# KV times wo for two head groups at once, in 64x64 TensorE tiles, on Trainium2

## The chip, the cores and the metric

The kernel runs on one core of a Trainium2 chip. The metric is device time in microseconds (us), the median of the runs. Five engines work side by side: TensorE (PE; its weight loads are listed as PEld), VectorE (DVE), ScalarE (ACT), GpSimd (POOL) and SyncE (SP), which here only issues DMAs.

## The reference, cut to what matters

One transformer block with adaptive layernorm: a linear attention block and a gated feed-forward block, on 2048 tokens of width 1024, 32 heads of 32, feed-forward width 3584, all bf16.

```python
mod = (_silu(c) @ w_mod).reshape(c.shape[0], 6, 1, -1)
sa, ca, ga, sb, cb, gb = (mod[:, 0], ..., mod[:, 5])
h = _layernorm(x) * (1 + ca) + sa
# A: linear attention
q, k, v = split of h @ wqkv into 32 heads of 32
phi = lambda t: jnp.where(t > 0, t + 1, jnp.exp(t)) + 1e-06
pq, pk = (phi(q), phi(k))
kv = jnp.einsum('bhsd,bhse->bhde', pk, v)
z = jnp.einsum('bhsd->bhd', pk)
num = jnp.einsum('bhqd,bhde->bhqe', pq, kv)
den = jnp.einsum('bhqd,bhd->bhq', pq, z)[..., None] + 1e-06
x = x + ga * ((num / den) @ wo)
# B: feed-forward
h = _layernorm(x) * (1 + cb) + sb
x = x + gb * (_gelu(h @ w_gate) * (h @ w_up) @ w_down)
```

## The kernel before, in words

The 32 heads stand in 8 groups of four, 128 columns each. The kernel never forms `num`. It multiplies each group's masked 128x128 KV matrix by the group's 128 rows of `wo` (already scaled by `ga`) and gets W2, 8 tiles of 128x1024. The attention output of a chunk of 128 tokens is then the scaled `pq` times W2, summed over the 8 groups (`wo_mm`, L1266).

The stages, in the order of TensorE:

1. Up to about 127 us: layernorm, the `k` and `q` products and `phi` of both.
2. The M stage, about 127 to 191 us. M is `pk`-transposed times the normalised input, 24 tiles (`m_tile`, L895) of 341 or 342 columns, accumulated over 16 chunks in PSUM banks 0 to 3 in turn. A DMA transpose (`m_t`, `mT`) turns a group's M, and `kv_prod` (L913) multiplies it by the group's columns of `wv` into bank 4 or 5. VectorE masks the result with the block-diagonal `BMASK` into `KVT` (L917). `w2_pair` (L1196) multiplies `KVT` by `WO` into two banks, two matmuls of 128x512, and ScalarE copies both banks to `W2` (L1198). Beside that `wofold` (L1202) scales `WO` by `GAB`, a broadcast row of modulation values; `den` (L1223, bank 5) gives the denominators, whose reciprocals go through DRAM and come back broadcast as `RB` (`rb_load`, L1243); `pq_scale` (L1256, notes `ps`) multiplies them into `pq`. `mod_rows` (L840) sums modulation rows over the partitions with a 32-column stationary operand, at four column positions, in bank 5 or 6.
3. The tail of the M stage, about 191 to 204 us: the first three token chunks of `wo_mm` (banks 0 and 1, 2 and 3, 4 and 5) are written out by hand between the last `kv_prod` and `w2_pair` calls.
4. The rest of `wo_mm` up to about 255 us, partly between feed-forward products. After a chunk, VectorE adds it to `x` (L1274), ScalarE and GpSimd make the second layernorm, and a DMA transpose brings it to the layout of the feed-forward products.
5. The feed-forward products (L1440) and the down projection (L1654), to the end.

`HOOK` puts named steps behind numbered M tiles: `kv3` is `kv_prod` of group 3, `w3` a `w2_pair`, `modp` the modulation rows of the second block, `gbr` the row of `gb`, `rb0.0` a load of `RB`.

The order on TensorE and on SP is the order in which the program is written. For VectorE, ScalarE and GpSimd, `reorder` is a planner over stages 1 to 3 (from the last `k` products to where the feed-forward code begins). It simulates all engines with `COST` (occupation and latency, looked up by the letters of an operation's note, (0.3, 0.1) where there is none), works out due times from the end back, and orders these three engines by due time among what is ready. A stream runs strictly in its order on the chip. DMAs of SP use 8 semaphores in turn, so each waits for the eighth before it.

`WO` lies where `wq` was, and `W2` where `wv` was. Before, `wo` comes in two loads of four groups each.

Of the kernel before, what the change touches and what calls it, by code (L numbers as in the profile page):

```python
# [18 lines left out]
NG = 8  # L19
# [24 lines left out]
OFF_WK = OFF_YT  # L44
# [126 lines left out]
class Sched:  # L171
# [41 lines left out]
    def dma(self, stream, fn, rd=(), wr=(), deps=(), note="", overwrite_ok=False):  # L213
# [6 lines left out]
        if prev is not None:  # L220
# [110 lines left out]
def bass_adaLN_cond__linear_attn_block__geglu_ffn__prompt_kernel(  # L331
# [18 lines left out]
    with ExitStack() as es:  # L350
# [30 lines left out]
        W2 = at("w2", [P, NG, D], bf16, OFF_WK)  # L381
# [63 lines left out]
        def r_sm(name):  # L445
            return [(SMO[name], SMO[name] + SMSZ[name], name)]
# [33 lines left out]
        def r_wo(g, c0=0, c1=D):  # L480
            return [(OFF_WQ + g * 2048 + c0 * 2, OFF_WQ + g * 2048 + c1 * 2, "wo")]
# [22 lines left out]
        def r_w(off, name, dc, c0=0, c1=D):  # L504
            return [(off + (dc * D + c0) * 2, off + (dc * D + c1) * 2, name)]
# [46 lines left out]
        sch = Sched()  # L552
# [356 lines left out]
        def kv_prod(g, bank):  # L909
            i = g % 2  # L910
            o = None
            for dc in range(NDC):
                o = sch.op(T, lambda e, dc=dc: e.matmul(PS(bank, 0, P), WV[:, g, dc, :], MTB[i][:, dc, :],  # L913
                                                        start=(dc == 0), stop=(dc == NDC - 1)),
                           rd=r_wv(g) + r_mtb(i), pwr=(pr(bank) if dc == 0 else ()), note=f"kv g{g} dc{dc}")
            pset_writer(bank, o)
            sch.op(V, lambda e: e.tensor_tensor(KVT[:, g, :], PS(bank, 0, P), BMASK[:, :], ALU.mult), prd=pr(bank), rd=r_sm("bmask"),  # L917
                   wr=r_kvt(g, g + 1), note=f"kvt{g}")

        bank_i = [0, 4]  # L920

# [268 lines left out]
            sch.op(V, lambda e: e.tensor_tensor(Z32[:], BM32[:], ZCOLS[:, :].unsqueeze(2).to_broadcast([P, NG, NH]), ALU.mult),  # L1190
                   rd=r_sm("bm32") + r_sm("zcols"), wr=r_sm("z32"), note="z32")

        def w2_pair(g, b0=6):
            for half in range(2):
                b = b0 + half
                sch.op(T, lambda e, b=b, half=half: e.matmul(PS(b), KVT[:, g, :], WO[:, g, half * 512:(half + 1) * 512], start=True, stop=True),  # L1196
                       rd=r_kvt(g, g + 1) + r_wo(g, half * 512, (half + 1) * 512), pwr=pr(b), note=f"w2 {g}.{half}")
            sch.op(A, lambda e: e.activation(W2[:, g, :], ps_all[:, b0 * 512:(b0 + 2) * 512], ACTF.Copy),  # L1198
                   prd=pr(b0) + pr(b0 + 1), wr=r_w(OFF_WK, "w2", g), note=f"w2cp{g}")
# [61 lines left out]
        def wo_mm(c_, b0, gs):  # L1261
            sg, ci = divmod(c_, CPG)
            last = [None, None]
            for g in gs:
                for half in range(2):
                    last[half] = sch.op(T, lambda e, g=g, half=half: e.matmul(  # L1266
                        PS(b0 + half), PQ[sg][:, g, ci * P:(ci + 1) * P], W2[:, g, half * 512:(half + 1) * 512],
                        start=(g == 0), stop=(g == NG - 1)),
                        rd=r_pq(sg, g, g + 1, ci * P, (ci + 1) * P) + r_w(OFF_WK, "w2", g, half * 512, (half + 1) * 512),
                        pwr=(pr(b0 + half) if g == 0 else ()), note=f"wo c{c_} g{g} h{half}")  # L1270
# [39 lines left out]
        for n, (g, k) in enumerate(tiles):  # L1310
# [656 lines left out]
```

## Time and profile before

| what | before |
|---|---|
| median of 3 runs | 783.46 us (783.44 to 783.54) |
| the profiled execution: time, span of its records | 783.52 us, 781.7 us |
| granted TensorE clock | 1.00 |
| PE busy | 774.5 us, 99% of the span |
| DVE busy | 641.9 us, 82% |
| ACT busy | 376.3 us, 48% |
| L1196 (KVT times WO) | 16 matmuls of 128x512, first at 149.3 us, last at 200.7 us |
| L917 (mask) | 8 instructions of 128x128, median 286 ns |
| L1202 (fold of `ga` into wo) | 8 instructions of 128x1024, median 1218 ns |
| L1205 (wo loads) | 2 of 1024 KB, 7.8 us to landing |
| VectorE busy between 120 and 205 us | 65.4 us |

Times within the execution count from the start of its span. Matmuls are pipelined: a matmul's listed duration reaches into the next one, so what one costs is read from one start to the next.

### The profile page before, as it was taken

The page shows a single profiled execution, that of the slowest core. Times are in us where ns is not written, and L with a number is a line of the kernel's source. Part 1 is how long each engine was busy: PE and PEld are TensorE (multiplying, and loading weights), DVE is VectorE, ACT ScalarE, POOL GpSimd, SP SyncE. Part 2 cuts the span into 40 slices and gives each one's busy share as a digit, 9 for nine tenths or more (in the row PEclk, how much of TensorE's full clock was granted, in tenths as well). Part 3 has the DMA queues.
Part 4 walks back from the last instruction along what each step waited for, and adds up shares of the span by engine and source line. Part 5 has one row for each costly group of instructions (what it writes and reads, how often), then busy time and mean ns, then how long its engine had stood idle before and what let it go on. Part 6 is the DMA issues. An engine that isn't in the chain of part 4 may idle for free.

```text
span 781.7 us, 10762 instructions
## 1 busy us (share of the span) xinstructions
PE 774.5 (99%) x3867; PEld 497.4 (64%) x3867; DVE 641.9 (82%) x954; ACT 376.3 (48%) x631; POOL 47.0 (6%) x126
## 2 busy tenths in 40 slices
PE   8999999999999999999999999999999999999998
PEld 4444445666445667677676767677676576677766
DVE  6699988896689877787989888888989888676767
ACT  2497743243566487778655565555555211111111
POOL 2031300000331012100000000000000000000000
DMA  9879749939999247867353866435356334444331
GB/s 289 250 166 252 156 84 260 229 70 182 216 270 248 82 128 215 226 184 214 93 152 107 246 207 180 141 102 160 94 150 218 112 115 152 145 141 123 113 128 60
DMA packets 196844, 130.22 MB, mean 167 GB/s; under 512 B 69420, under 2 KB 182324, under 8 KB 195768
## 3 DMA queue, kind: packets, MB, share of 16 engines
q1 hardware_dynamic: 196776, 129.55, 61.0%
q8 instruction: 30, 0.49, 0.3%
q14 instruction: 22, 0.18, 0.1%
q10 hardware_dynamic: 16, 0.00, 0.0%
HBM read 92.55 MB, written 23.35 MB: 148 GB/s over the span
## 4 chain that ended last, share of the span: by engine, by line
PE 97%; SPq 1%; DMA 1%; DVE 0%; issue 0%; DVEq 0%
PE ps_all L1440 45%; PE ps_all L1654 21%; PE ps_all L895 7%; PE ps_all L1266 7%; PE ps_all L931 7%; PE ps_all L880 6%; PE ps_all L1575 1%; DMA wmq<-in_w_mod_dram 1%; SPq L598 1%; SPq L603 1%; PE ps_all L913 0%; PE ps_all L1196 0%; SPq L592 0%; PE ps_all L1223 0%; PE ps_all L766 0%; PE ps_all L840 0%
## 5 line engine op out<-in xcount | busy, mean ns | idle before, releaser
L1440 PE MATMUL ps_all<-ss,tp 128*128 128x512 f32 x896 | 214.3, 396 | 0.0
L1440 PEld LDWEIGHTS ps_all<-ss,tp 128*128 128x128 f32 x896 | 168.3, 188 | 37.7 <-DVE ss L1395 0.3
L1654 PE MATMUL ps_all<-dt,sb 128*128 128x512 f32 x424 | 102.5, 398 | 0.0
L1440 PE MATMUL ps_all<-h2a,wt 128*128 128x512 bf16 x448 | 101.6, 380 | 0.0
L1463 ACT ACTIVATE ge<-ps_all 128x512 f32<-128x512 f32 x112 | 64.1, 597 | 73.8 <-DVE ps_all L1451 62.0
L1654 PEld LDWEIGHTS ps_all<-dt,sb 128*128 128x128 f32 x424 | 79.6, 188 | 18.4 <-DVE sb L1630 0.3
L1458 DVE TENSOR_TENSOR ps_all<-ps_all,es 128x512 f32<-128x512 f32 x54 | 37.5, 699 | 49.7 <-ACT es L1448 49.3
L1470 DVE TENSOR_TENSOR ys<-ge,ps_all 128x512 bf16<-128x512 f32 x112 | 74.4, 684 | 3.4 <-PE ps_all L1654 0.5
L1440 PEld LDWEIGHTS ps_all<-h2a,wt 128*128 128x128 bf16 x448 | 37.9, 97 | 57.2 <-ACT ps_all L1445 16.9
L1415 DVE TENSOR_TENSOR tp<-wt 128x1024 fp32r<-128x1024 bf16 x56 | 68.1, 1216 | 2.1 <-DMA wt<-in_B_w_up_dram 2.1
L1415 DVE TENSOR_TENSOR tp<-wt,tp 128x1024 fp32r<-128x1024 bf16 x56 | 68.2, 1219 | 0.0
L880 PE MATMUL ps_all<-wk,h1T 128*128 128x512 bf16 x248 | 56.7, 379 | 0.3 <-DVE h1T L724 0.2
L931 PE MATMUL ps_all<-h1T,wq 128*128 128x512 bf16 x256 | 56.7, 379 | 0.0
L1266 PE MATMUL ps_all<-w,pq 128*128 128x512 bf16 x256 | 56.3, 379 | 0.0
L1440 PE MATMUL ps_all<-ar,tp 128*128 128x512 f32 x224 | 55.5, 390 | 0.0
L869 ACT ACTIVATE eb<-ps_all 128x512 f32<-128x512 f32 x64 | 36.3, 593 | 37.7 <-PE ps_all L880 15.3
L1654 PE MATMUL ps_all<-wd,ya 128*128 128x512 bf16 x212 | 48.5, 380 | 0.0
L1440 PEld LDWEIGHTS ps_all<-ar,tp 128*128 128x128 f32 x224 | 42.1, 188 | 8.8
L1445 ACT ACTIVATE ps_all<-ps_all 128x512 f32<-128x512 f32 x56 | 32.6, 582 | 27.1 <-PE ps_all L1440 27.1
L931 PEld LDWEIGHTS ps_all<-h1T,wq 128*128 128x128 bf16 x256 | 24.9, 98 | 30.0
L1266 PEld LDWEIGHTS ps_all<-w,pq 128*128 128x128 bf16 x256 | 24.7, 98 | 29.9 <-ACT w L1198 0.3
L1625 ACT ACTIVATE sb<-ya 128x896 fp32r<-128x896 bf16 (+1 forms) x16 | 14.5, 913 | 58.8 <-PE ps_all L1654 58.8
(140 smaller groups left out, 977.5 us busy)
## 6 DMA issues: line engine op xcount, KB each, us to landing
wt<-in_B_w_gate_dram SPq DMA_DIRECT2D x28, 512.0 KB, 4.1
wt<-in_B_w_up_dram SPq DMA_DIRECT2D x28, 512.0 KB, 5.3
scr_y<-ys SPq DMA_DIRECT2D x28, 512.0 KB, 3.2
ya<-scr_y SPq DMA_DIRECT2D x14, 896.0 KB, 5.9
rb<-scr_rd SPq DMA_DIRECT2D x32, 256.0 KB, 6.9
wd<-in_B_w_down_dram SPq DMA_DIRECT2D x7, 1024.0 KB, 7.9
wmst<-in_w_mod_dram SPq DMA_DIRECT2D x6, 1024.0 KB, 5.7
wmq<-in_w_mod_dram SPq DMA_DIRECT2D x8, 512.0 KB, 6.8
```

Of the source, the lines that this page charges most:

```text
L869: sch.op(A, lambda e: e.activation(EB[i][:, :], PS(bank), ACTF.Exp), prd=pr(bank), wr=rng, note=f"{note}.exp")
L880: o = sch.op(T, lambda e, dc=dc: e.matmul(PS(bank), H1[sg][:, ci, dc, :], W_[:, dc, jg * 512:(jg + 1) * 512], start=(dc == 0), stop=(dc == ...
L895: o = sch.op(T, lambda e, c_=c_: e.matmul(PS(bank, 0, n), PK[c_][:, g * P:(g + 1) * P], xrow(c_, o_, o_ + n), start=(c_ == 0), stop=(c_ == ...
L931: o = sch.op(T, lambda e, dc=dc: e.matmul(PS(b), WQ[:, dc, qc * P:(qc + 1) * P], H1[sg][:, :, dc, :], start=(dc == 0), stop=(dc == NDC - 1 ...
L1266: last[half] = sch.op(T, lambda e, g=g, half=half: e.matmul(PS(b0 + half), PQ[sg][:, g, ci * P:(ci + 1) * P], W2[:, g, half * 512:(half + ...
L1415: sch.op(V, lambda e: e.tensor_tensor(TP[k][:], in0, in1 if k in (0, 2) else in1[:], ALU.subtract), rd=r0 + r1, wr=r_tp(k), deps=[x1_ops[7 ...
L1440: o = sch.op(T, lambda e, l_=l_, r_=r_, dc=dc: e.matmul(PS(b), l_, r_, start=fresh and dc == 0, stop=dc == ND2 - 1, skip_group_check=True) ...
L1445: sch.op(A, lambda e: e.activation(PS(BB + t), PS(BA + t), ACTF.Copy), prd=pr(BA + t), pwr=pr(BB + t), note="pcp")
L1458: sch.op(V, lambda e: e.tensor_tensor(PS(BC + t), PS(BC + t), ES[t][:, :], ALU.add), prd=pr(BC + t), rd=r_2k(OFF_ES[t], f"es{t}"), pwr=pr( ...
L1463: sch.op(A, lambda e: e.activation(GE[i][:, :], PS(b), ACTF.Gelu_apprx_tanh), prd=pr(b), wr=r_2k(OFF_GE[i], f"ge{i}"), note="gelu")
L1470: sch.op(V, lambda e: e.tensor_tensor(YS[s_][:, 2 * h:2 * h + 2, t, :], q(GE[i][:, :]), q(PS(b + 1)), ALU.mult), rd=r_2k(OFF_GE[i], f"ge{i ...
L1654: o = sch.op(T, lambda e, l_=l_, r_=r_, j=j, dst=dst: e.matmul(dst, l_[:, 0, :], r_, start=(k in (1, 5) or own is not None) and j == js[0] ...
```

## The change

The 128x128 KV matrix of a group is block-diagonal with blocks of 32, so only its two 64x64 diagonal blocks are kept. A `kv_prod` now writes these two with two VectorE instructions, into one half of the partitions of `KVT`: an even group into partitions 0 to 63, an odd one into 64 to 127; slot 2i holds the upper blocks of groups 2i and 2i+1, slot 2i+1 the lower blocks. The rows of `wo` are loaded in the same arrangement, by four loads of 64 partitions.

`w2_pair(i)` does groups 2i and 2i+1 at once: eight matmuls with 64 rows, 64 columns and 512 moving columns each. Row half r belongs to group 2i+r and goes to banks 4+2r and 5+2r, column half h to partitions 64h to 64h+63. ScalarE copies both results, except that for i of 2 and 3 VectorE copies the odd group's. There are four such calls instead of eight: behind M tiles 11 and 17 (counted from 0) and twice in the tail. `modp` moves from tile 14 to tile 15, and the chunks of `wo_mm` in the tail are cut differently. In `COST`, the entries `w`, `kvt` and VectorE's `wcp` are new values, and the loads' new note `woe` has no entry.

```diff
-              "modr": (0.04, 0.15), "mod": (0.028, 0.15), "w": (0.216, 0.15), ...
+              "modr": (0.04, 0.15), "mod": (0.028, 0.15), "w": (0.07, 0.3), ...
-               ... "kvt": (0.21, 0.085), ...
+               ... "kvt": (0.15, 0.085), ... "wcp": (1.05, 0.085), ...
 def kv_prod(g, bank):
...
-            sch.op(V, lambda e: e.tensor_tensor(KVT[:, g, :], PS(bank, 0, P), BMASK[:, :], ALU.mult), ...)
+            z = 64 * (g % 2)
+            for h in range(2):
+                a, gz = 64 * h, g // 2 * 2 + h
+                sch.op(V, lambda e, a=a, gz=gz: e.tensor_tensor(KVT[z:z + 64, gz, 0:64], ps_all[a:a + 64, bank * 512 + a:bank * 512 + a + 64], BMASK[a:a + 64, a:a + 64], ALU.mult), ...)
...
-        def w2_pair(g, b0=6):
-            for half in range(2):
-                b = b0 + half
-                sch.op(T, lambda e, b=b, half=half: e.matmul(PS(b), KVT[:, g, :], WO[:, g, half * 512:(half + 1) * 512], start=True, stop=True), ...)
-            sch.op(A, lambda e: e.activation(W2[:, g, :], ps_all[:, b0 * 512:(b0 + 2) * 512], ACTF.Copy), ...)
+        def w2_pair(i, b0=4):
+            for hf in range(2):
+                for r in range(2):
+                    for h in range(2):
+                        b, g = b0 + 2 * r + hf, 2 * i + h
+                        sch.op(T, lambda e, b=b, g=g, h=h, r=r, hf=hf: e.matmul(ps_all[64 * h:64 * h + 64, b * 512:(b + 1) * 512], KVT[64 * r:64 * r + 64, g, 0:64],
+                               WO[64 * r:64 * r + 64, g, hf * 512:(hf + 1) * 512], start=True, stop=True), ...)
+            for r in range(2):
+                b, g = b0 + 2 * r, 2 * i + r
+                w_, p_ = W2[:, g, :], ps_all[:, b * 512:(b + 2) * 512]
+                eng = V if i > 1 and r else A
+                sch.op(eng, lambda e, w_=w_, p_=p_, eng=eng: e.activation(w_, p_, ACTF.Copy) if eng == A else e.tensor_copy(w_, p_), ...)
 def wofold(kc):
+    ... deps=wo_ops[2 * (kc % 2) + 1:2 * (kc % 2) + 2] ...
+        WO4 = WO[:].rearrange("p (i h) d -> p i h d", h=2)
+        wo_rows = A_wo.rearrange("(i r h p) d -> r p i h d", r=2, h=2, p=64)
         def wo_load(j):
-            sch.dma(Q, lambda e: e.dma_start(WO[:, 4 * j:4 * j + 4, :], wo_v[:, 4 * j:4 * j + 4, :]), ...)
+            for r in range(2):
+                wo_ops.append(sch.dma(Q, lambda e, r=r: e.dma_start(WO4[64 * r:64 * r + 64, :, j, :], wo_rows[r, :, :, j, :]), ... note="woe"))
...
-        HOOK = {0: "ga", 6: "kv0", 8: "w0", 9: "kv1", 11: "w1", 12: "kv2", 14: "w2 modp", 15: "kv3 z32", 16: "den0", 17: "w3 rb0.0 rb0.1", 18: "",
-                19: "kv4", 20: "w4 den1 ps0.0", 21: "gbr", 22: "ps0.1", 23: "rb2.0"}
+        HOOK = {0: "ga", 6: "kv0", 9: "kv1", 11: "w0", 12: "kv2", 15: "modp kv3 z32", 16: "den0", 17: "w1 rb0.0 rb0.1", 18: "",
+                19: "kv4", 20: "den1 ps0.0", 21: "gbr", 22: "ps0.1", 23: "rb2.0"}
...
-        wo_mm(0, 0, E6[:5])
-        w2_pair(5)
-        kv_prod(6, 4)
-        wo_mm(1, 2, E6[:5])
-        kv_prod(7, 5)
-        w2_pair(6)
-        wo_mm(0, 0, E6[5:])
-        wo_mm(1, 2, E6[5:])
+        wo_mm(0, 0, [0, 1, 2, 3])
+        w2_pair(2)
+        wo_mm(1, 2, [0, 1, 2])
+        kv_prod(6, 4)
+        kv_prod(7, 5)
+        wo_mm(0, 0, [4, 5])
         rb_load(1)
         rb_load(2, (1,))
-        wo_mm(2, 4, E6[:4])
-        w2_pair(7)
-        wo_mm(2, 4, E6[4:])
+        w2_pair(3)
+        wo_mm(1, 2, [3, 4, 5])
+        wo_mm(2, 4, list(range(6)))
         for c_ in range(3):
             wo_mm(c_, 2 * c_, [6, 7])
```

More of the change, by code (lines that the diff above doesn't have):

```diff
@@ L227 @@
         PE_: {"T": (0.056, 0.15), "k": (0.216, 0.15), "q": (0.216, 0.15), "v": (0.216, 0.15), "m": (0.145, 0.15), "kv": (0.056, 0.15), "den": (0.027, 0.15),
-              "modr": (0.04, 0.15), "mod": (0.028, 0.15), "w": (0.216, 0.15), "wo": (0.216, 0.15), "ffn": (0.216, 0.15)},
+              "modr": (0.04, 0.15), "mod": (0.028, 0.15), "w": (0.07, 0.3), "wo": (0.216, 0.15), "ffn": (0.216, 0.15)},
         ACT_: {"exp": (0.5, 0.1), "sum": (1.19, 0.1), "sq": (1.28, 0.1), "xhata": (1.14, 0.1), "hmoda": (0.49, 0.1), "mcp": (0.38, 0.1), "zc": (0.13, 0.1),
@@ L232 @@
         DVE_: {"min": (0.34, 0.085), "add": (0.607, 0.085), "bn": (0.603, 0.085), "aggr": (0.124, 0.085), "ve": (0.07, 0.085), "xhat": (0.46, 0.085),
-               "nm": (0.074, 0.085), "hmod": (0.25, 0.085), "macc": (0.66, 0.085), "mlo": (0.6, 0.085), "kvt": (0.21, 0.085), "z": (0.34, 0.085),
-               "dene": (0.335, 0.085), "rden": (1.67, 0.085), "pqs": (0.6, 0.085), "wofold": (1.13, 0.085), "x": (1.14, 0.085), "ssum": (1.15, 0.085), "tsum": (1.15, 0.085), "padd": (0.62, 0.085), "yT": (0.62, 0.085)},
+               "nm": (0.074, 0.085), "hmod": (0.25, 0.085), "macc": (0.66, 0.085), "mlo": (0.6, 0.085), "kvt": (0.15, 0.085), "z": (0.34, 0.085),
+               "dene": (0.335, 0.085), "wcp": (1.05, 0.085), "rden": (1.67, 0.085), "pqs": (0.6, 0.085), "wofold": (1.13, 0.085), "x": (1.14, 0.085), "ssum": (1.15, 0.085), "tsum": (1.15, 0.085), "padd": (0.62, 0.085), "yT": (0.62, 0.085)},
         POOL_: {"nmean": (0.22, 0.05), "ve": (0.22, 0.05), "rstd": (0.55, 0.05), "nm": (0.55, 0.05), "ones": (0.12, 0.05), "ssum": (2.3, 0.05), "tsum": (2.3, 0.05)},
@@ L916, in kv_prod @@
             pset_writer(bank, o)
-            sch.op(V, lambda e: e.tensor_tensor(KVT[:, g, :], PS(bank, 0, P), BMASK[:, :], ALU.mult), prd=pr(bank), rd=r_sm("bmask"),
-                   wr=r_kvt(g, g + 1), note=f"kvt{g}")
+            z = 64 * (g % 2)
+            for h in range(2):
+                a, gz = 64 * h, g // 2 * 2 + h
+                sch.op(V, lambda e, a=a, gz=gz: e.tensor_tensor(KVT[z:z + 64, gz, 0:64], ps_all[a:a + 64, bank * 512 + a:bank * 512 + a + 64], BMASK[a:a + 64, a:a + 64], ALU.mult),
+                       prd=pr(bank), rd=r_sm("bmask"), wr=r_kvt(gz, gz + 1), note=f"kvt{g}", overwrite_ok=True)
         bank_i = [0, 4]
@@ L1191, in z32 @@
                    rd=r_sm("bm32") + r_sm("zcols"), wr=r_sm("z32"), note="z32")
-        def w2_pair(g, b0=6):
-            for half in range(2):
-                b = b0 + half
[L1196 to L1199, printed above, removed]
+        def w2_pair(i, b0=4):
[4 more added lines that the diff above has]
+                        sch.op(T, lambda e, b=b, g=g, h=h, r=r, hf=hf: e.matmul(ps_all[64 * h:64 * h + 64, b * 512:(b + 1) * 512], KVT[64 * r:64 * r + 64, g, 0:64],
+                               WO[64 * r:64 * r + 64, g, hf * 512:(hf + 1) * 512], start=True, stop=True),
+                               rd=r_kvt(g, g + 1) + r_wo(g, hf * 512, (hf + 1) * 512), pwr=pr(b), note=f"w2 {i}.{hf}", overwrite_ok=True)
+            for r in range(2):
+                b, g = b0 + 2 * r, 2 * i + r
+                w_, p_ = W2[:, g, :], ps_all[:, b * 512:(b + 2) * 512]
+                eng = V if i > 1 and r else A
+                sch.op(eng, lambda e, w_=w_, p_=p_, eng=eng: e.activation(w_, p_, ACTF.Copy) if eng == A else e.tensor_copy(w_, p_),
+                       prd=pr(b) + pr(b + 1), wr=r_w(OFF_WK, "w2", g), note=f"w2cp{g}")
@@ L1201, in wofold @@
         def wofold(kc):
-            sch.op(V, lambda e: e.tensor_tensor(WO[:, kc, :], WO[:, kc, :], GAB[:, :], ALU.mult), rd=r_wo(kc) + R_GAB, wr=r_wo(kc), note=f"wofold {kc}")
+            sch.op(V, lambda e: e.tensor_tensor(WO[:, kc, :], WO[:, kc, :], GAB[:, :], ALU.mult), rd=r_wo(kc) + R_GAB, wr=r_wo(kc), deps=wo_ops[2 * (kc % 2) + 1:2 * (kc % 2) + 2], note=f"wofold {kc}")
+        wo_ops = []
+        WO4 = WO[:].rearrange("p (i h) d -> p i h d", h=2)
+        wo_rows = A_wo.rearrange("(i r h p) d -> r p i h d", r=2, h=2, p=64)
@@ L1204, in wo_load @@
         def wo_load(j):
-            sch.dma(Q, lambda e: e.dma_start(WO[:, 4 * j:4 * j + 4, :], wo_v[:, 4 * j:4 * j + 4, :]),
-                    wr=[t_ for g in range(4 * j, 4 * j + 4) for t_ in r_wo(g)], note=f"wo{j}")
+            for r in range(2):
+                wo_ops.append(sch.dma(Q, lambda e, r=r: e.dma_start(WO4[64 * r:64 * r + 64, :, j, :], wo_rows[r, :, :, j, :]),
+                                      wr=() if r else [t_ for g in range(j, NG, 2) for t_ in r_wo(g)], deps=wo_ops[-1].deps if r else (), note="woe"))
@@ L1328, in bass_adaLN_cond__linear_attn_block__geglu_ffn__prompt_kernel @@
                 hook_run(f)
-        E6 = list(range(6))
-        wo_mm(0, 0, E6[:5])
-        w2_pair(5)
+        wo_mm(0, 0, [0, 1, 2, 3])
+        w2_pair(2)
+        wo_mm(1, 2, [0, 1, 2])
         kv_prod(6, 4)
-        wo_mm(1, 2, E6[:5])
         kv_prod(7, 5)
-        w2_pair(6)
-        wo_mm(0, 0, E6[5:])
-        wo_mm(1, 2, E6[5:])
+        wo_mm(0, 0, [4, 5])
         rb_load(1)
         rb_load(2, (1,))
-        wo_mm(2, 4, E6[:4])
-        w2_pair(7)
-        wo_mm(2, 4, E6[4:])
+        w2_pair(3)
+        wo_mm(1, 2, [3, 4, 5])
+        wo_mm(2, 4, list(range(6)))
         for c_ in range(3):
```

## The prediction

> **What bounds the kernel now.** First the page's busy times and its chain that ended last, to see which engine sets the end.
>
> ```profile
> PE 774.5 (99%) x3867; PEld 497.4 (64%) x3867; DVE 641.9 (82%) x954; ACT 376.3 (48%) x631; POOL 47.0 (6%) x126
> ...
> PE 97%; SPq 1%; DMA 1%; DVE 0%; issue 0%; DVEq 0%
> ```
>
> TensorE is busy for 774.5 of 781.7 us and carries 97% of the chain. So an edit counts by the TensorE time that it takes away or adds, and by the new waits that it gives TensorE; work on other engines is free until TensorE waits for it.
>
> Then the timeline of TensorE where the changed product (L1196) runs, once beside a row reduction in column tiles (L840) and once in the tail.
>
> ```profile
> 164.71 0.45 PE L895 MATMUL ps_all<-xall,pk 128*128 128x341 bf16 x2
> 165.00 0.59 PE L1196 MATMUL ps_all<-wo,kvt 128*128 128x512 bf16 x2
> 165.52 0.62 PE L840 MATMUL ps_all<-hl,ones 128*32 128x512 bf16 x8
> 166.07 0.32 PE L895 MATMUL ps_all<-xrow,pk 128*128 128x341 bf16 x1
> ...
> 200.48 0.59 PE L1196 MATMUL ps_all<-wo,kvt 128*128 128x512 bf16 x2
> 200.91 41.60 PE L1266 MATMUL ps_all<-w,pq 128*128 128x512 bf16 x192
> ```
>
> Starts tell the cost, since matmuls overlap their neighbours. A pair of L1196 takes 200.91 - 200.48 = 0.43 us, or 0.216 for one matmul of 512 columns. The eight of L840 are just as wide, and 8 x 0.216 = 1.73, but they take only 0.64, from 165.43 (where the pair before them is through) to 166.07. So four column tiles run side by side: two rounds of 0.216, plus about 0.21 for going into the tiled shape and back.
>
> Then VectorE in the tail and where the feed-forward products begin, for the waits near the path.
>
> ```profile
> 189.73 2.50 DVE L1256 TENSOR_TENSOR pq<-pq,rb 128x512 bf16<-128x512 bf16 x4 [0.77 <-DMA rb<-scr_rd]
> 192.14 0.28 DVE L917 TENSOR_TENSOR kvt<-ps_all,bmask 128x128 bf16<-128x128 f32 x1
> 195.05 0.29 DVE L917 TENSOR_TENSOR kvt<-ps_all,bmask 128x128 bf16<-128x128 f32 x1 [2.63 <-PE ps_all L913]
> 197.66 0.29 DVE L917 TENSOR_TENSOR kvt<-ps_all,bmask 128x128 bf16<-128x128 f32 x1 [2.31 <-PE ps_all L913]
> 200.90 1.89 DVE L1256 TENSOR_TENSOR pq<-pq,rb 128x512 bf16<-128x512 bf16 x3 [2.96 <-DMA rb<-scr_rd]
> ...
> 225.33 1.22 DVE L1415 TENSOR_TENSOR tp<-wt 128x1024 fp32r<-128x1024 bf16 x1 [2.11 <-DMA wt<-in_B_w_up_dram]
> ...
> 251.65 1.21 DVE L1395 TENSOR_TENSOR ss<-h2a,h2b 128x1024 fp32r<-128x1024 bf16 x1
> ```
>
> And TensorE's timeline at the same place:
>
> ```profile
> 252.92 2.12 PE L1440 MATMUL ps_all<-ss,tp 128*128 128x512 f32 x8
> ```
>
> In the tail VectorE has 7.9 us idle (2.63 + 2.31 + 2.96). From 225.33 it is busy almost without a break up to 252.86, and 0.06 later TensorE begins a product that reads what it has just written. There the two engines are level: a gain made at 200 us survives only if VectorE's chain moves up too.
>
> **The W2 product.** Removed: 8 pairs x 0.433 (the mean of the six pairs that a full-array matmul follows) = 3.46 us. Added: 4 calls of eight 64x64 matmuls, 512 columns each, four tiles at a time. No row of before has 64-row tiles. From below, a call is two bare rounds, 0.43. From above, the eight run one after another, 1.73 + 0.21 = 1.94. I take the nearest row, L840's 0.64: same width, same count, four tiles at once, a shape change on both sides. 4 x 0.64 = 2.56, so TensorE loses 0.90 us, all on the path: 5 pairs less and 2 calls more before the last M tile (-0.88), 3 pairs less and 2 calls more in the tail (-0.02).
>
> The L840 and L1223 rows also decide whether weights load beside running matmuls: the 32 of L1223 (128x256) start at 171.26 and the next group at 172.25, so eight rounds in 0.99 hide four loads each, all on the same 128 rows. [...]
>
> **Mask (L917).** One 128-column instruction of 0.28 becomes two of 64 columns, 0.14 to 0.28 each: up to 2.2 us more on VectorE over the stage, which has 19.6 us idle in 120 to 205. It counts only before a W2 call, below.
>
> **Copies of W2.** ACT loses two of its 1.02 us copies to VectorE, where the nearest row (x1, 128x1024 from PSUM) is 1.22. They fall at 193.4 and 197.1, into the idle time shown.
>
> **Loads of wo.** Two of 1024 KB become four of 512 KB: the same bytes, two more issues on SP (0.46 to 2.47 each by the two there now). Behind them are the store of the modulation row (130.90) and the load of gab (136.94), which the first wofold awaits at 140.94; the last wo byte lands at 129.46 + 7.8 = 137.3. At worst the folds come some 5 us late. The first W2 call now stands at the 12th M tile (about 154 us), so this cover holds.
>
> **Moves in M.** modp goes one tile later: its input was ready at 165.37 for a start at 165.52, and now gets 2.3 us more. Its store left SP at 170.44 behind a weight load at 169.97, so the later start delays nothing in that queue. The call after the 18th tile writes bank 5 once VectorE has read den0 from it (172.64 + 0.42, against 174.59): 1.5 us spare. kv2 needs bank 4 one tile after the first call: the copy is over 1.76 after the call's start, kv2 comes at 2.96.
>
> **The tail, with kv5 over at 191.81 - 0.88 = 190.93.** Matmul counts x 0.216, kv 0.44, call 0.64:
> - call 2 at 192.66 needs kvt5. VectorE's scaling ends at 192.14 at the latest, plus two masks 192.42 to 192.70: level at worst, 0.5 spare if rb also comes earlier.
> - kv6 at 194.59 needs bank 4. The call's matmuls end 0.71 after its start, ACT's copy takes 1.02: free at 194.42, spare 0.17.
> - kv7 at 195.03 needs its transpose, issued at 192.09 - 0.88 and landing 3.1 later, 194.3: spare 0.7.
> - call 3 at 196.34 needs kvt7: 195.64 + at most 0.56, spare 0.14.
> - chunk 2 at 198.27 needs banks 4 and 5 again: 198.10, spare 0.17.
> - W2[7] is wanted at 201.3, its copy ends at 198.3.
>
> These margins are thin: I book no wait, and up to 0.3 for the range. What comes after (rb loads, first x1, transposes, wt load) hangs on the transpose of group 7 and on TensorE, both 0.88 earlier, so VectorE's chain to 252.86 moves up too.
>
> **Sum.** The profiled execution took 783.52 (span 781.7 and 1.8 around it). 783.52 - 0.90 = 782.62; the median of the three runs is 0.06 lower, so 782.6.
>
> **Rivals.**
> - *Gain eaten at 252.9.* If rb's landing (200.90), wt's (225.33) or the planner's new VectorE order holds that chain in place, TensorE waits there for the 0.9 it saved: 783.5. For it: 0.06 us of slack. Against: both loads hang on events that move up.
> - *Tiles of one row half run in turn* (slower). Every round of four becomes two matmuls in turn, each behind its own load of about 0.096 (L840's and L1196's loads): 2 x (0.216 + 0.096) = 0.62 for 0.216, 0.41 more in 8 rounds = +3.3. With the 0.9 saved, +2.4: 785.9. It decides from 0.11 us more per round on. Against it stand L840 and L1223, though with 32-column tiles over all rows. [...]
> - *VectorE's order turns.* The planner sees new costs (wo loads now fall to its default of 0.3, 0.1), and could put the scaling of the second row group, which waits for rb, ahead of the copy of W2[7]. rb lands at 200.0, four scalings of 0.6 end at 202.4, the copy at 203.7; TensorE wanted it at 201.3 and waits 2.4: 785.0. Against: the copy is ready almost 3 us before rb lands.
> - *The shape is not used:* the matmuls run one by one, 4 x 1.94 = 7.8 against 3.46: 787.8.
> - *More than forecast:* no cost for the change of shape (-1.74 us) gives 781.7.
>
> **Chances.** Forecast 0.60 (its own range 782.4 to 783.0), eaten 0.15, tiles in turn 0.08, order turned 0.10, shape not used 0.03, more than forecast 0.04. A measurement of this kernel tells about 0.2% (1.57 us) from no change. Slower than that: 0.08 + 0.03 and a little less than half of the order's 0.10, 0.15 in all. Faster than that: most of 0.04, 0.03. The rest, 0.82, is within. The range leaves out the tiles in turn, the shape not used and half of the turned order above, and little below: 782.0 to 785.0.
>
> **What would show it.** Right: the L1196 rows in 64x64 with four starts close together, 0.64 from the last full matmul to the next; L895 after the last tile 0.9 earlier; L913 and L1266 in the tail with no idle before them; the L1440 product of 252.92 at about 252.0. Wrong: a second start of a round 0.2 or more after the first (tiles in turn); idle on TensorE near 192.7, 194.6 or 201 with DVE or ACT as releaser; VectorE's ss at 251.65 not moved.

## The result, and the profile after

The changed kernel takes 784.88 us (median of 15 runs, 783.62 to 786.29). The kernel before, run beside it on the same chip, takes 783.44 (15 runs, 783.14 to 783.76). The ratio is 1.0018, with a 95% interval of 1.0011 to 1.0026: slower, by about 1.4 us, where 0.9 us less was forecast. The profiled execution of after took 784.34 us, with a span of 782.5, which is 0.8 more than before's 781.7.

First the busy times and the chain that ended last, of after.

```profile
PE 774.6 (99%) x3883; PEld 496.0 (63%) x3883; DVE 645.6 (83%) x964; ACT 374.4 (48%) x629; POOL 47.5 (6%) x126
...
PE 92%; DMA 3%; SPq 2%; DVE 1%; issue 0%; ACT 0%; DVEq 0%; ACTq 0%
```

TensorE's share of the chain falls from 97% to 92%, and DMA and the issue queue of SP rise from 1% each to 3% and 2%. So more of the chain runs over transfers than before; what that costs TensorE is read from its waits below. The new code has other line numbers: the W2 product is L1201 (L1196 before), the mask L920, the copies of W2 L1208, the fold of `wo` L1212, its load L1220, `wo_mm` L1281, the feed-forward product L1452. L895 (M tiles) and L913 (`kv_prod`) keep theirs.

The timeline of TensorE in after, at the first W2 call and at the first call of the tail. Columns: start, time, engine, line, operation, tile and shape, count.

```profile
157.93 0.63 PE L1201 MATMUL ps_all<-wo,kvt 64*64 64x512 bf16 x8
158.49 1.19 PE L895 MATMUL ps_all<-xrow,pk 128*128 128x341 bf16 x7
...
194.37 0.63 PE L1201 MATMUL ps_all<-wo,kvt 64*64 64x512 bf16 x8
194.93 1.47 PE L1281 MATMUL ps_all<-w,pq 128*128 128x512 bf16 x6
```

The M tile ahead of the first call is through at 157.84 (its last matmul of 342 columns starts at 157.695, plus 0.145), and M goes on at 158.49: 0.65 us a call, where 0.64 was booked. In the records of that call the four matmuls of a round start within 0.01 us, and the second round starts 0.24 us behind the first.

So the saving is there, and something else has eaten it. The waits of TensorE name it. These three lines are of after; before has no wait at L913 at all.

```profile
PE ps_all L913 <- DMA mtb<-mb: 0.6, 1, 0.6
PE ps_all L913 <- ACT w L1208: 0.3, 1, 0.3
PE ps_all L913 <- issue: 0.2, 1, 0.2
```

`mtb` is the transposed M, which `kv_prod` multiplies by `wv`. On TensorE's timeline of after the three are the first three `kv_prod`, each behind nine M matmuls:

```profile
142.88 1.47 PE L895 MATMUL ps_all<-xall,pk 128*128 128x341 bf16 x9
144.53 0.61 PE L913 MATMUL ps_all<-mtb,wv 128*128 128x128 bf16 x8 [0.18 <-issue]
...
150.64 1.47 PE L895 MATMUL ps_all<-xall,pk 128*128 128x341 bf16 x9
152.74 0.62 PE L913 MATMUL ps_all<-mtb,wv 128*128 128x128 bf16 x8 [0.63 <-DMA mtb<-mb]
...
159.52 1.47 PE L895 MATMUL ps_all<-xall,pk 128*128 128x341 bf16 x9
161.28 0.61 PE L913 MATMUL ps_all<-mtb,wv 128*128 128x128 bf16 x8 [0.29 <-ACT w L1208]
```

Nine M matmuls take 9 x 0.145 = 1.31, so `kv0` could have started at 144.19, `kv1` at 151.95 and `kv2` at 160.83. They start 0.34, 0.79 and 0.45 later: 1.58 us, against the 0.9 saved. (The brackets give less, since a matmul's modelled end reaches beyond the next start.)

Why the transposes are late stands in the issue queue of SP. First before, then after:

```profile
126.90 3.02 SPq L1205 DMA_DIRECT2D wo<-in_A_wo_dram  x2
130.90 0.64 SPq L849 DMA_DIRECT2D scr_row<-mrowa  x1
136.94 0.35 SPq L855 DMA_DIRECT2D gab<-scr_row  x1
137.39 1.29 SPq L703 DMA_TRANSPOSE mtb<-mb  x1
138.78 1.88 SPq L595 DMA_DIRECT2D wmst<-in_w_mod_dram  x2
142.63 2.49 SPq L703 DMA_TRANSPOSE mtb<-mb  x1
```

```profile
127.52 2.82 SPq L1220 DMA_DIRECT2D wo<-in_A_wo_dram  x4
130.87 0.62 SPq L849 DMA_DIRECT2D scr_row<-mrowa  x1
139.38 0.35 SPq L855 DMA_DIRECT2D gab<-scr_row  x1
139.84 1.31 SPq L703 DMA_TRANSPOSE mtb<-mb  x1
141.24 1.85 SPq L595 DMA_DIRECT2D wmst<-in_w_mod_dram  x2
143.18 5.23 SPq L703 DMA_TRANSPOSE mtb<-mb  x1
```

The store of the modulation row leaves at the same time in both. SP stands until it has landed, since the gab load reads what it wrote (SP's waits, before and then after):

```profile
SPq L855 <- DMA scr_row<-mrowa: 5.3, 1, 5.3
```

```profile
SPq L855 <- DMA scr_row<-mrowa: 7.8, 1, 7.8
```

The gab load leaves 2.44 us later in after, and the transposes of M stand behind it. The second transpose starts only 0.55 us later than before, but its issue takes 5.23 us instead of 2.49. In both traces that issue ends within 0.2 us of the landing of the first of the two weight loads (`wmst`) ahead of it: 145.1 us before, 148.5 after. These loads, too, left 2.46 us later, behind the gab load, so `kv1` pays by the same queue; why the issue ends just there is not shown. The transposes land at 144.4 and 152.7, just before `kv0` and `kv1` start, so the wait that the profile calls "issue" is one for a transpose too.

The store travels behind the bytes of `wo`: SP goes on at 136.94 and 139.38, and the last byte of `wo` lands at 137.3 and 139.7. The same 2 MB take longer, as the windows of the two kernels show (columns: stretch, length, busy times of PE, PEld, DVE, ACT, POOL, granted clock, DMA share, GB/s; before, then after):

```profile
132.00:134.00 2.00, 2.00 (x16) 1.34 (x14) 2.00 (x4) 0.46 (x1) 0.00 (x0) 1.00 0.94 350
134.00:136.00 2.00, 2.00 (x16) 1.31 (x15) 2.00 (x4) 0.87 (x2) 0.00 (x0) 1.00 1.05 407
```

```profile
132.00:134.00 2.00, 2.00 (x16) 1.34 (x14) 2.00 (x4) 0.46 (x1) 0.00 (x0) 1.00 1.07 215
134.00:136.00 2.00, 2.00 (x16) 1.33 (x14) 2.00 (x5) 0.90 (x2) 0.00 (x0) 1.00 1.08 225
136.00:138.00 2.00, 2.00 (x16) 1.32 (x15) 2.00 (x5) 0.65 (x4) 0.00 (x0) 1.00 1.07 223
```

The DMA engines are busy nearly all the time in both (shares of 0.94 to 1.08), but the loads of 64 partitions move 215 to 225 GB/s where those of 128 move 350 to 407. A packet of 2048 bytes takes 160 ns instead of 84 (medians of the packets that start from 132 to 136 us). Experiment 2 asks whether the number of loads does this, experiment 3 whether it is how many partitions or which; by what means, no run shows.

The wait of `kv2` begins with the late gab load too, two steps on. VectorE stood for gab (first line), its sums for the modulation came late, ScalarE stood for those, and the W2 copies that `kv2` needs bank 4 from are behind that on ScalarE (lines of VectorE, then ScalarE, of after):

```profile
143.33 2.36 DVE L1212 TENSOR_TENSOR wo<-wo,gab 128x1024 bf16<-128x1024 bf16 x2 [4.71 <-DMA gab<-scr_row]
```

```profile
159.59 0.63 ACT L825 ACTIVATE hl<-acc 128x512 bf16<-128x512 f32 x1 [1.03 <-DVE acc L819]
160.13 1.92 ACT L1208 ACTIVATE w<-ps_all 128x1024 bf16<-128x1024 f32 x2
```

In the tail VectorE has taken the copies where there was room, and the feed-forward product is 0.71 later than before's 252.92 (lines of VectorE, then TensorE, of after):

```profile
195.10 1.23 DVE L1208 CAST w<-ps_all 128x1024 bf16<-128x1024 f32 x1 [1.26 <-PE ps_all L1201]
196.90 0.99 DVE L920 TENSOR_TENSOR kvt<-ps_all,bmask 64x64 bf16<-64x64 f32 x4 [0.58 <-PE ps_all L913]
198.84 1.22 DVE L1208 CAST w<-ps_all 128x1024 bf16<-128x1024 f32 x1 [0.94 <-PE ps_all L1201]
201.50 1.90 DVE L1271 TENSOR_TENSOR pq<-pq,rb 128x512 bf16<-128x512 bf16 x3 [1.44 <-DMA rb<-scr_rd]
```

```profile
253.63 2.11 PE L1452 MATMUL ps_all<-ss,tp 128*128 128x512 f32 x8
```

### The profile page after: what moved, and what is told of

The parts are those of the page before. It is cut to its first block, busy times and chain, and to the rows that moved or that the text cites. A ratio compares the mean times of both kernels' runs of the same rounds, so it can differ in the third digit from the quotient of the medians.

```text
span 782.5 us, 10801 instructions
## 1 busy us (share of the span) xinstructions
PE 774.6 (99%) x3883; PEld 496.0 (63%) x3883; DVE 645.6 (83%) x964; ACT 374.4 (48%) x629; POOL 47.5 (6%) x126
## 2 busy tenths in 40 slices
DMA packets 196876, 130.22 MB, mean 166 GB/s; under 512 B 69452, under 2 KB 182356, under 8 KB 195800
## 4 chain that ended last, share of the span: by engine, by line
PE 92%; DMA 3%; SPq 2%; DVE 1%; issue 0%; ACT 0%; DVEq 0%; ACTq 0%
PE ps_all L1452 45%; PE ps_all L1666 21%; PE ps_all L1281 7%; PE ps_all L934 7%; PE ps_all L880 6%; PE ps_all L895 4%; PE ps_all L1587 1%; DMA wmst<-in_w_mod_dram 1%; SPq L598 1%; DMA scr_row<-mrowa 1%; DMA wmq<-in_w_mod_dram 1%; DVE acc L819 1%; SPq L603 1%; PE ps_all L913 0%; PE ps_all L1238 0%
## 5 line engine op out<-in xcount | busy, mean ns | idle before, releaser
L1452 PE MATMUL ps_all<-ss,tp 128*128 128x512 f32 x896 | 214.3, 396 | 0.0
L1452 PEld LDWEIGHTS ps_all<-ss,tp 128*128 128x128 f32 x896 | 168.2, 188 | 37.8 <-DVE ss L1407 0.2
L1452 PE MATMUL ps_all<-h2a,wt 128*128 128x512 bf16 x448 | 101.6, 380 | 0.0
L1452 PEld LDWEIGHTS ps_all<-h2a,wt 128*128 128x128 bf16 x448 | 38.0, 98 | 57.2 <-ACT ps_all L1457 16.9
L1281 PE MATMUL ps_all<-w,pq 128*128 128x512 bf16 x256 | 56.4, 379 | 0.0
L1452 PE MATMUL ps_all<-ar,tp 128*128 128x512 f32 x224 | 55.5, 390 | 0.0
L1452 PEld LDWEIGHTS ps_all<-ar,tp 128*128 128x128 f32 x224 | 42.1, 188 | 8.9
L1457 ACT ACTIVATE ps_all<-ps_all 128x512 f32<-128x512 f32 x56 | 32.6, 582 | 26.9 <-PE ps_all L1452 26.9
L1281 PEld LDWEIGHTS ps_all<-w,pq 128*128 128x128 bf16 x256 | 24.6, 98 | 30.2 <-issue 1.1
```

What stands on the lines that cost most here:

```text
L1281: last[half] = sch.op(T, lambda e, g=g, half=half: e.matmul(PS(b0 + half), PQ[sg][:, g, ci * P:(ci + 1) * P], W2[:, g, half * 512:(half + ...
L1452: o = sch.op(T, lambda e, l_=l_, r_=r_, dc=dc: e.matmul(PS(b), l_, r_, start=fresh and dc == 0, stop=dc == ND2 - 1, skip_group_check=True) ...
L1457: sch.op(A, lambda e: e.activation(PS(BB + t), PS(BA + t), ACTF.Copy), prd=pr(BA + t), pwr=pr(BB + t), note="pcp")
```

## The experiments

Theory A: the tiles save 0.9 us as forecast, and the slow half-partition loads of `wo` cost more than that, through what stands behind them. Rivals: it is the number of loads and not their shape; the new arrangement of tail and tiles costs the time itself; the planner's order does.

The work ahead of the M stage takes more or less time from run to run (L840's row reduction starts between 129.22 and 130.22 us in the records), so each kernel is read twice: by its median, and in its trace by the **stretch** from the start of L840's eight matmuls near 129.9 us to the start of the feed-forward product near 252.9. What follows that stretch took 528.8 to 529.3 us in every kernel. A stretch is one execution: experiment 4 ran twice and differs by 0.16, and in experiment 2 0.23 us were lost at the feed-forward product alone, so differences of a quarter of a microsecond are not read. Each median is of 4 to 15 runs, and each ratio is to the kernel before as it ran beside that one (medians of 783.38 to 783.57).

| kernel | median, us | ratio to before, 95% interval | stretch, us | against before |
|---|---|---|---|---|
| before | 783.44 | | 122.98 | |
| after | 784.88 | 1.0011 to 1.0026 | 123.73 | +0.75 |
| 1 before, loads halved | 785.02 | 1.0009 to 1.0027 | 124.72 | +1.74 |
| 2 before, four full loads | 783.77 | 0.9994 to 1.0012 | 123.23 | +0.25 |
| 3 before, cut at 32 and 96 | 783.86 | 0.9996 to 1.0015 | 123.37 | +0.39 |
| 4 after, full loads | 782.88 | 0.9985 to 1.0003 | 122.12 | -0.86 |
| 4 again | 783.08 | 0.9986 to 1.0003 | 122.28 | -0.70 |
| 5 after, planner's cost restored | 784.61 | 1.0008 to 1.0027 | 123.98 | +1.00 |
| 6 after, second pair later | 786.01 | 1.0016 to 1.0040 | 126.16 | +3.18 |
| 7 after, second pair later still | 788.01 | 1.0051 to 1.0082 | 127.44 | +4.46 |
| 8 after, gab load later | 784.93 | 1.0014 to 1.0034 | 124.43 | +1.45 |
| 9 after, halves on two queues | 785.66 | 1.0017 to 1.0041 | 125.33 | +2.35 |
| 10 after, `wo` reordered in DRAM | 783.26 | 0.9988 to 1.0006 | 122.82 | -0.16 |
| 11 after, eight loads | 815.54 | 1.0396 to 1.0424 | 155.58 | +32.60 |

The edits below are cut to the lines that matter; the dependences that go with them are left out.

**1. The loads alone, in the kernel before.** Nothing of the tiles, only each load cut into two halves of the partitions.

```diff
-  e.dma_start(WO[:, 4*j:4*j+4, :], wo_v[:, 4*j:4*j+4, :])
+  for r in range(2):
+      e.dma_start(WO[64*r:64*r+64, 4*j:4*j+4, :], wo_v[64*r:64*r+64, 4*j:4*j+4, :])
```

> The kernel before, with each of its two wo loads cut into two of 64 partitions (512 KB each); W2 and the order stay as before. Theory A (a load into half of the partitions runs at half the rate, and the store of the modulation row, the gab load and the transposes of M queue behind it): the store lands some 2.4 us later than before, kv0 and kv1 wait for their transposes, TensorE loses 0.8 to 1.5 us: 784.3 to 785.0. Theory B (the new order on VectorE and ScalarE, or the tiled product, is what costs): 783.5, no wait before L913.

The rate near 134 us falls to 221 to 229 GB/s, gab leaves SP at 139.51, and TensorE waits before `kv0` and `kv1`, as in after (lines of this kernel):

```profile
PE ps_all L913 <- issue: 0.7, 1, 0.7
PE ps_all L913 <- DMA mtb<-mb: 0.3, 1, 0.3
```

This edit by itself makes the kernel before slower, by as much as the whole change does. Its stretch is 1.74 longer, about what after's +0.75 and the 0.88 saved come to together, which leaves little or nothing for the new order of the rows in DRAM.

**2. Four loads over all partitions, in the kernel before.**

```diff
-  e.dma_start(WO[:, 4*j:4*j+4, :], wo_v[:, 4*j:4*j+4, :])
+  for k in (4*j, 4*j+2):
+      e.dma_start(WO[:, k:k+2, :], wo_v[:, k:k+2, :])
```

> The kernel before, with four wo loads of 512 KB, each over all 128 partitions and two groups. Theory A: the rate stays as it was, 783.5, no new wait. Theory C (four issues on SP in place of two, and their semaphore turns, are what delays the queue): as the kernel with loads of 64 partitions, 784.3 to 785.0.

As many loads of the same size as after has. gab leaves at 136.87, L913 doesn't wait, and the time can't be told from before's. So the number of loads isn't the cause.

**3. Which partitions, or how many.** Each load cut into partitions 32 to 95, 0 to 31, and 96 to 127.

```diff
-  e.dma_start(WO[:, 4*j:4*j+4, :], wo_v[:, 4*j:4*j+4, :])
+  for p0, p1 in ((32, 96), (0, 32), (96, 128)):
+      e.dma_start(WO[p0:p1, 4*j:4*j+4, :], wo_v[p0:p1, 4*j:4*j+4, :])
```

> The kernel before, with each 1 MB load of wo cut by partitions into 32 to 95 (512 KB), 0 to 31 and 96 to 127 (256 KB each). Is it the number of partitions or which of them that makes a load slow? [...] Theory P2 (how many: 64 partitions in one load are slow wherever they lie): all at 215 GB/s or less, 9.5 us or more, gab at 139.5 or later as in the cut at 64, and the time is 785 or more.

The windows of this kernel: in the first and third stretch the loads of 32 to 95 run, in the second and fourth the quarters.

```profile
129.50:130.50 1.00, 1.00 (x14) 0.52 (x13) 1.00 (x3) 0.71 (x3) 0.00 (x0) 1.00 1.00 389
131.00:133.00 2.00, 2.00 (x16) 1.34 (x14) 2.00 (x4) 0.46 (x1) 0.00 (x0) 1.00 1.05 228
133.50:134.50 1.00, 1.00 (x9) 0.66 (x8) 1.00 (x3) 0.00 (x0) 0.00 (x0) 1.00 1.05 358
135.00:136.50 1.50, 1.50 (x12) 0.97 (x11) 1.50 (x4) 0.88 (x2) 0.00 (x0) 1.00 1.00 213
```

Sixty-four partitions across the middle go at 358 to 389 GB/s, as fast as 128, and the quarters at 213 to 228. So it is which partitions a load reaches, not how many. gab leaves at 137.76, where the halves of experiment 1 let it go at 139.51, and only `kv1` still waits, 0.2 us.

**4. The change with full loads.** `wo` in two loads over 128 partitions, in the row order of before, so the tiles meet other rows of `wo` than the reference's product would. Everything else is the change.

```diff
-  for r in range(2):
-      e.dma_start(WO4[64*r:64*r+64, :, j, :], wo_rows[r, :, :, j, :])
+  e.dma_start(WO4[:, :, j, :], A_wo.rearrange("(i h p) d -> p i h d", h=2, p=P)[:, :, j, :])
```

> The changed kernel, with wo loaded by two loads over all 128 partitions in the old row arrangement; the rows that W2 is made of are then other rows, so what it computes differs, the work does not. Theory A: no wait before L913, the whole 0.9 us of the tiled product comes through: 782.6. Theory B: as the changed kernel, 784.9.

> The changed kernel with wo loaded in the order of before (so other rows of wo meet the tiles than the reference wants), by two transfers of 1 MB over 128 partitions: the same as in the first such run, again beside the version above. Theory A: 782.5 to 783.0, within 0.3 us of the version with eight loads; if the eight issues cost something on SyncE, that version is 0.3 us or more behind this one.

L913 waits nowhere, gab leaves at 135.35, and the stretch is 0.86 and 0.70 shorter than before's. Both ratios are 0.9994, about 0.5 us under before, though each interval reaches just over 1, so the gain itself is shown by the traces and not by a verdict of the times. Against after it is 1.8 to 2.0 us by the medians. That clears the tiles, the tail and the mask: the loss is in the loads. (The version with eight loads that the second text compares with is experiment 11.)

**5. The planner.** The wo loads are given the note for which the planner has a cost.

```diff
-  note="woe"
+  note="wo"
```

> The changed kernel, with the four wo loads given to the planner under the name for which it has a cost (0.45 and 2.7 us) instead of its default (0.3 and 0.1). Theory A: the planner's order has no part in the loss; the waits of L913 stay near 1.1 us and the time is 784.4 to 785.4. Rival (the order that came from the default cost delays the copies or the folds): the wait of L913 for the W2 copy at 161 us goes and the time is 784.0 or less.

The wait of `kv2` for the W2 copy goes, as the rival wanted, but `kv1` waits longer (start by start 1.01 instead of 0.79), 0.34 us are lost at the feed-forward product, and the time stays. The planner's order moves a part of the loss about; it isn't its source.

**6, 7, 8. The same slow bytes in another place.** Three ways to get what is urgent ahead of them: the second pair of loads behind the gab load (6); behind the second transpose of M, with the folds reordered (7); or the gab load itself behind the first transpose and, in the trace, one of the two weight loads that follow it, with the folds three tiles later (8).

```diff
 # 6
-  wo_load(0); wo_load(1)
+  wo_load(0)          # wo_load(1) behind the gab load
 # 7
+  if n == 5: wo_load(1)
-  wofold(n - 2)
+  wofold((0, 2, 4, 6, 1, 3, 5, 7)[n - 2])
 # 8
-  HOOK = {0: "ga", 6: "kv0", ...
+  HOOK = {0: "ga", 2: "gal", 6: "kv0", ...      # gal: the gab load
-  if 2 <= n <= 9:  wofold(n - 2)
+  if 5 <= n <= 12: wofold(n - 5)
```

> The changed kernel, with the second pair of wo loads issued behind the store of the modulation row and the load of gab (1 MB is ahead of the store in place of 2). Theory A: the store lands at about 133.7 in place of 139.3, gab some 3 us earlier than even in the kernel before, the transposes of M in time: 782.6 to 783.0. If instead the fold of wo is what is late (the second pair now lands later, about 142 us), kv and W2 calls wait for VectorE: 784.9 or more.

> The changed kernel, with the second pair of wo loads issued after the first two transposes of M, and the fold of wo in the order 0 2 4 6 1 3 5 7, so that the folds that need the second pair come last. Theory A (what counts is what stands ahead of the transposes of M): half of the slow bytes are ahead of them, so kv0 and kv1 do not wait, and the time is 782.5 to 783.2, if the transposes that follow find the queue free. Rival (the slow bytes cost as much wherever they stand in the M stage): waits of 0.5 us or more move to kv1 or kv2, 783.8 to 785.

> The changed kernel with its slow wo loads as they are, but with the load of gab issued behind the first transpose of M and the two weight loads that follow it, and the folds of wo three tiles later. It computes the reference. Theory A (the loss comes from SyncE, which stands at the gab load until the modulation row's store has come through behind the slow bytes, with the transposes of M queued behind it): the first transpose leaves SyncE by 138 us instead of 139.8, kv0 does not wait, the second transpose lands no later than before, the wait of L913 at kv1 is under 0.4 us, VectorE does not stand at the first fold, and the time is 782.5 to 783.5. Rival (the DMA engines' backlog is what counts, whatever the order of issue): the transposes land as late as in the changed kernel, L913 waits about 1 us in all, and the time is 784.3 or more.

All three missed what theory A said of them. In 6 the gab load leaves early, at 134.53, but the second pair now stands between it and the first transpose, which leaves at 136.39 and lands 9.76 us later; `kv0` waits over 2 us. In 7 both transposes are in time, but the second pair lands so late that VectorE stands at the fold that needs it, with the mask and the modulation sums behind it; this is that line of VectorE, and then TensorE's wait at `kv2`:

```profile
153.94 1.23 DVE L1212 TENSOR_TENSOR wo<-wo,gab 128x1024 bf16<-128x1024 bf16 x1 [5.91 <-DMA wo<-in_A_wo_dram]
```

```profile
162.50 0.63 PE L913 MATMUL ps_all<-mtb,wv 128*128 128x128 bf16 x8 [2.39 <-ACT w L1208]
```

In 8 the first transpose leaves at 135.34 and `kv0` doesn't wait, but the gab load stands on SP up to 143.21, with the second weight load and the second transpose behind it. That transpose lands at 153.33, and `kv1` waits (line of that kernel):

```profile
153.38 0.62 PE L913 MATMUL ps_all<-mtb,wv 128*128 128x128 bf16 x8 [1.88 <-DMA mtb<-mb]
```

Experiment 8 is not a clean test of the order. In its trace VectorE has another order ahead of the M stage as well, and the loads of `wo` leave at 129.46 instead of 127.52, which makes everything behind them later.

So my first picture, that only SP's stand at the gab load hurts, was too narrow. In after's windows of 2 us from 130 to 156 us the DMA engines are full (shares of 1.04 to 1.35) but for 138 to 142, where SP stands (0.22 and 0.70). As I read the three runs, the longer time of the slow loads is added to a backlog, and the order of issue chooses who pays; that no order would hide it is not shown.

**9. The two halves on two queues.** Partitions 64 to 127 issued by ScalarE.

```diff
-  sch.dma(Q, ...)
+  sch.dma(A if r else Q, ...)
```

> The changed kernel, with the two loads of wo for partitions 64 to 127 issued by ScalarE, the two for partitions 0 to 63 by SyncE as before, so that the halves are in two queues and can be under way together. [...] Theory A2 (the halves are served in turn whatever the queue): the rate stays at 215 to 240 GB/s, the waits of L913 stay near 1 us and the time is 784.5 to 785.5.

The rate is 209 to 226 GB/s from 128 to 136 us and reaches 290 only in 136 to 138; the last byte of `wo` lands at 140.28, as in after (139.68), and the time is no better. Each half alone is slow, and for most of the time the two rates don't add up.

**10. The order made in DRAM.** Near 100 us four copies within DRAM put `wo` into the order of the tiles; two loads over 128 partitions follow.

```diff
+  for n in range(4):      # r = n % 2, h = n // 2
+      e.dma_start(wo_scr[r, :, :, h, :], wo_rows[r, :, :, h, :])
-  for r in range(2): ...
+  e.dma_start(WO[:, 4*j:4*j+4, :], scr_wo[:, 4*j:4*j+4, :])
```

> The changed kernel, with wo first copied within DRAM, near 100 us, into the order that the 64x64 tiles want, by four transfers of 512 KB, and then loaded by two transfers of 1 MB over all 128 partitions. It computes the reference. Theory A: the loads run at 350 GB/s or more, gab leaves SyncE by 137 us, no wait of L913 on TensorE, and the 0.9 us of the W2 product stays: 782.4 to 783.0, faster than both kernels. Rival: the four copies share the DMA engines with the x loads and their writes near 100 us, and that delays something TensorE waits for: above 783.4.

The loads run at 361 to 434 GB/s in 130 to 134 us, gab leaves at 135.68, L913 doesn't wait: the loss is undone, by 1.6 us against after. Of the gain 0.16 us is left in the stretch. TensorE stands 0.46 us by starts at the feed-forward product, for VectorE (line of this kernel):

```profile
252.66 1.66 PE L1455 MATMUL ps_all<-ss,tp 128*128 128x512 f32 x6 [0.29 <-DVE ss L1410]
```

It can't be told from the kernel before, so none of the versions that do the whole computation beats it.

**11. The order made by the load itself.** Eight loads of one head group each over all 128 partitions, the DRAM side read as 2 x 64 rows.

```diff
-  for r in range(2):
-      e.dma_start(WO4[64*r:64*r+64, :, j, :], wo_rows[r, :, :, j, :])
+  for g in range(j, NG, 2):
+      e.dma_start(WO[:, g, :], wo_rows[:, :, g // 2, j, :])
```

> The changed kernel, with wo loaded in the same new order, but by eight transfers of 256 KB (one head group each, all 128 partitions) instead of four of 512 KB (64 partitions each). It computes the reference. Theory A (partitions per load, and what stands on SyncE behind it): 2048-byte packets go at 350 GB/s or more, the eight issues take about 5 us on SyncE and push the store of the modulation row from 130.9 to about 132.5, gab leaves SyncE by 138 us, L913 waits less than 0.3 us in all, and the time is 782.4 to 783.2: faster than the kernel before by 0.3 to 1 us. Rival: the issues on SyncE cost what the bandwidth gains, gab leaves at 139 or later and the time is 784 to 785.

Both theories missed by 30 us. The load reaches all partitions, yet moves 51 GB/s (window and wait of this kernel):

```profile
132.00:134.00 2.00, 2.00 (x16) 1.32 (x14) 2.00 (x4) 0.46 (x1) 0.00 (x0) 1.00 0.13 51
```

```profile
PE ps_all L913 <- issue: 31.4, 1, 31.4
```

Behind that wait the eight matmuls of `kv_prod` take 0.81 us by starts, and the seven and nine M matmuls that follow 1.99 and 1.47; in after, at `kv0`, they take 0.44, 1.02 and 1.30. So about 1.5 of the 32.6 us are a slower TensorE (the mean granted clock of this execution was 0.981). A DMA share of 0.13 is the time of two of the sixteen engines (0.13 x 16 = 2.1), and a packet of 2048 bytes then takes an estimated 0.13 x 16 x 2048 bytes / 51 GB/s = 84 ns, as in the loads of before. The packets were not slower; too few were under way at once. What held them back is not shown: beside the four full loads of experiment 2 these differ in their DRAM side and in their size, 256 KB for 512.

## Why the prediction was wrong, step by step

- **TensorE bounds, an edit counts by TensorE's time and waits:** right.
- **The W2 product, 0.64 a call:** right, 0.65. The 64x64 tiles run four at a time and keep their weight loads hidden (32 loads of 102 to 106 ns; the eight of the first call start within 0.04 us, and none shows in the 0.65). The rival's tiles in turn would have made it 1.46 (0.64 + 2 x 0.41). The four calls of after do not run so: in each the second round starts 0.24 us behind the first.
- **Loads of wo: the step that failed.** I wrote "the same bytes" and took the same time for them, and asked only who waits for the folds. Two things were wrong. The bytes took longer: 215 to 225 GB/s, so the gab load left 2.44 us later. And the cover that I named, the first W2 call at the 12th tile, covers the folds alone: the first fold came 2.4 us late (143.33 for 140.94), and no W2 call waited. ("About 154 us" for that call was misread; by before's rows it stands at 157.16 - 0.43 = 156.7, which gives only more cover.) Behind the gab load on SP stand the transposes of M, which `kv_prod` needs at 144.2 and 152 us. They were in the trace of before, at 137.39 and 142.63, and I left them out. Sized by starts: +1.58 us on TensorE, where I had booked nothing. With the -0.88 saved up to the last M tile that is +0.70, and the stretch shows +0.75. The trace of before held the warning too: the loads of `rb`, each over one quarter of the partitions, move 209 to 225 GB/s in its windows of 194 to 200 us.
- **The mask:** two of 0.22 to 0.23, inside the bounds. **The copies on VectorE:** 1.23 at 195.10 and 198.84, in idle time, as placed.
- **Bank 4 for `kv2`, "the copy is over 1.76 after the call's start":** wrong by the same cause. It took until 161.28, since ScalarE was held up by late modulation sums. With full loads (experiment 4) `kv2` doesn't wait; with the planner's other order (experiment 5) it doesn't either, so the slow loads and that order make this wait together.
- **The tail:** right. From `kv5`'s start, call 2 comes 2.27 us later, `kv6` 4.16, call 3 6.00, where the steps give 2.17, 4.10 and 5.85. Of each call's delay about 0.09 is the way into the tiled shape, which the 0.64 counts inside the call; behind call 3 the next chunk starts at 6.56 for 6.49, so the thin margins have cost 0.07.
- **VectorE's order turns:** it didn't. The copy at 198.84 is ahead of the scaling at 201.50.
- **Gain eaten at 252.9:** in after there was no gain to eat. Where it came through, 0 and 0.09 us of it were lost there in experiment 4, 0.46 in experiment 10. The rival was real, and in part the reason why even a repaired version shows so little.
- **The sum:** with full loads it comes out as -0.86 and -0.70 for -0.90. The forecast was right for the edit that its title names, and wrong for the load that the edit needs.
- **The range, 782.0 to 785.0:** 784.88 lies inside it by luck. The room above was meant for a turned order and thin margins; that the load itself could get slower is in none of the terms and none of the rivals.

What stays open: the medians of before and after differ by 1.4 us, the two profiled executions by 0.8. The runs of after spread over 2.7 us and those of before beside them over 0.6, as they would if a chain of transfers of varying length is now exposed. But in the later comparisons the runs of before spread over 1.3 to 2.9 us, and only one execution of after is recorded, so this is not shown.

## What to carry to other kernels

An edit that changes how data must lie on the partitions changes the load that brings it: price the load anew, by which partitions it reaches and how its DRAM side is read, from rows of the same shape, and not by its bytes (the same 2 MB went at 350 to 407 GB/s, at 215 to 225, and at 51 in experiment 11). Then read the issue queue behind it to the end, past the first waiter, to each transfer that the bounding engine needs soon. Here, with the DMA engines nearly full (shares of 1.04 to 1.35 from 130 to 156 us, but for 138 to 142), three ways of moving the slow load did not hide it; two loads over all partitions (experiments 4 and 10) did away with it.

## What the runs showed of the hardware that was not expected

- A load over partitions 0 to 63 or 64 to 127 moves 215 to 229 GB/s, one over 32 to 95 358 to 389, one over 128 350 to 434. Two halves issued on two queues at once moved 209 to 226 for most of the time, 290 at best.
- The eight loads of experiment 11, 128 partitions and 256 KB each with the DRAM side read as 2 x 64 rows, move 51 GB/s, with a DMA share of 0.13, and their issues on SP take 0.54 to 7.15 us each, with a median of 4.97.
- In experiment 7, behind TensorE's stand of 2.4 us, the granted clock fell to 0.74, 0.50 and 0.91 in the three windows of 2 us from 162 to 168. By the clock's loss, 2 x (0.26 + 0.50 + 0.09), that is an estimated 1.7 us on top of the wait. Behind the waits of 2.0 us in experiment 6 and 1.9 in experiment 8 no such loss shows: there the seven M matmuls behind `kv_prod` take 1.02 us by starts, in experiment 7 1.98.
